# An RWKV layer and its FFN on one core: the last chunk of the opening is made in the FFN's own rows, its low parts by TensorE, with a new order of the first 32 tasks

## The chip, the cores and the metric

One core of one Trainium2 chip runs the whole program. The metric is the device time of one execution in microseconds (us); lower is better. Each kernel is executed several times, and one further execution is profiled. In that one the hardware profiler writes down when each instruction of each engine began and ended.

## The reference

There are two parts. A recurrence over 768 tokens runs for 4 batches and 8 heads of 48 channels; its output, 3072 tokens by 384 channels, is the input `x` of a feed-forward network (FFN) with 2048 hidden channels.

```python
def _attn_ref(r, k, v, w, u):
    ...
    for t in range(S):
        kt, vt, rt, wt = (k[:, :, t], v[:, :, t], r[:, :, t], w[:, :, t])
        cur = np.einsum('bhd,bhe->bhde', u[None] * kt, vt)
        y[:, :, t] = np.einsum('bhd,bhde->bhe', rt, state + cur)
        state = wt[:, :, :, None] * state + np.einsum('bhd,bhe->bhde', kt, vt)

def _moe_ref(x, w_in, w_out):
    h = x @ w_in
    g = h * (1.0 / (1.0 + np.exp(-1.702 * h)))
    return (g @ w_out).astype(np.float32)
```

## The kernel before

**Chunks.** The recurrence is cut into 24 chunks of 128 tokens, six to a batch. A chunk (`chunk(t)`, one `a` token of the order a step) takes these steps. VectorE makes running products of the decays, forward (`pm`) and backward (`li`), by two scans, and from them the scaled keys and queries `kf` and `qf` (both in the tile `kq`). TensorE makes the diagonal term (`ps_d`, from the product `rku` of r and k), the transposed keys (`ps_t`), the state's increment (`ps_u`), the scores (`ps_e` or `ps_s`) and the output `ps_y`. That output is the sum of a product of the queries with the state (L460) and a product of the masked scores `am` with the values (L507). `split` then writes the output into the FFN's input tile `x` as a high part (ScalarE, L229) and a low part (VectorE, L230, the output less its high part). ScalarE also squares `lp` (both running products) and `kq` and adds them up (`measure`, L235; the `m` tokens); the sums are tested at the end, and a guarded slow path runs if a value is out of range. `convert` (the `w` tokens) turns a fetched megabyte of 64-bit weights into a pair of a high and a low part: two ScalarE steps (L209, L210), two VectorE steps (L212, L215), one ScalarE step (L218), one VectorE step (L220).

**Tasks.** The FFN works through 96 tasks: six groups of four chunks (512 tokens), each with 16 slices of 128 hidden channels. A task j has a first product `g` of nine matmuls (three row blocks, each high by high, high by low, low by high), a gelu `h` on ScalarE and VectorE, and a second product `y` of nine matmuls into three accumulators `po`. The first product's result `ph` has two banks, so the task after the next waits until a gelu has read its bank.

**Rows.** An output `ps_y` has 112 rows: two heads of 48 channels with 16 rows between them, for four pairs of heads. The FFN wants three blocks of 128 rows. `fill_x` (the `x` tokens) closes that gap with six DMAs of 16 rows each inside `x` (L526), three issued by SyncE (SP) and three by GpSimd (POOL) in the opening.

**Order.** Nothing is scheduled by a tool. The string `RAMP` lists all steps of the first 32 tasks, and each engine gets its instructions in that order; `rest()` does the same for the steady part by the table `PARTS`. In `RAMP`, a token is a letter and a number: `l` loads a chunk, `f` fetches weights, `M` writes small constants, and `kN` issues N dummy matmuls on zeros (`keep_clock`, L602), which keep TensorE active. SyncE's queue takes its DMAs in that order too; `behind_moves` makes the DMAs issued after the six moves wait until the moves have landed.

Of the kernel before, what the change touches and what calls it, by code (L numbers as in the profile page):

```python
# [8 lines left out]
F32 = mybir.dt.float32  # L9
# [5 lines left out]
ALU = mybir.AluOpType  # L15
# [37 lines left out]
PARTS = [("a", 0, 0), ("a", 1, 0), ("a", 2, 0), ("m", 2, 0), ("a", 2, 1), ("a", 3, 0), ("m", 3, 0), ("a", 3, 1), ("a", 4, 1),  # L53
         ("a", 4, 1), ("l", 5, 0), ("l", 5, 0), ("a", 5, 1), ("a", 5, 1), ("a", 8, 1), ("a", 8, 1), ("x", 8, 1)]
BEFORE = 11

# [19 lines left out]
HALF = 14  # L76
WP = NF * DM // NL
# [8 lines left out]
def rwkv_ffn_kernel(ctx: ExitStack, tc, wkr, vp, vrk, ub, w_in, w_out, masks, vt, uc, out):  # L86
# [35 lines left out]
    later_b = later.bitcast(I32).unsqueeze(1).broadcast_to([P, NP, HB])  # L122
    u_heads = hm[:, 2:].rearrange("r (p h) -> r p h", h=2)
# [77 lines left out]
    def convert(i, pool, clamp):  # L201
# [6 lines left out]
        sums = {} if clamp else dict(accum_out=acc[:, 2 * NT + i : 2 * NT + i + 1])  # L208
# [43 lines left out]
    def token_halves(t, kf, qf, kt, v, s, sf):  # L252
# [78 lines left out]
        for b, y in enumerate(ps):  # L331
            split(*(xs[i][0:R2, n_, :, cols][:, :, half[b]] for n_ in range(2)), y)
# [3 lines left out]
    def chunk(t):  # L336
# [23 lines left out]
        if t < WHOLE:  # L360
            rk = at.tile([R2, NP, C], F32, tag="rku", name="rku")
# [11 lines left out]
        measures[t] = measured(t, lp, kq)  # L373
# [6 lines left out]
        if t < WHOLE:  # L380
            V.tensor_copy(s, ps_d.rearrange("p n h -> p (n h)"))
# [82 lines left out]

        if t < CHUNKS[0]:
# [458 lines left out]
```

## Time and profile before

| what | value |
|---|---|
| time, median of 3 runs | 502.7 us (502.22 to 502.75) |
| the profiled execution's own time | 502.98 us |
| its span in the trace | 501.2 us, 1.78 us less than its own time |
| busy: TensorE (PE) / VectorE (DVE) / ScalarE (ACT) / GpSimd (POOL) | 490.2 / 285.0 / 279.7 / 82.3 us |
| instructions in the trace | 12797 |
| dummy matmuls in the order | 79 |

The profile lists PE (matmuls), PEld (weight loads), DVE, ACT and POOL; a name with a q (SPq) is the engine's queue issuing a DMA. A span of the trace is a little shorter than the time of its execution, so sums made in the trace are carried over to the execution's own time, and from there to the median of the runs.

### The profile page before, as it was taken

To read this page: it belongs to the slowest core of one execution; us is meant where nothing else is said; L and a number is where in the kernel's file an instruction comes from. 1 tells how busy PE (TensorE), PEld (TensorE's weight loads), DVE (VectorE), ACT (ScalarE), POOL (GpSimd) and SP (SyncE) were. 2 spreads that over 40 slices of the span, in tenths; PEclk is the share of its full clock that TensorE was granted. 3 is DMA by queue.
4 is the path that set the end of the run, shared out by engine and by line. 5 is a ranking of instruction groups with operands and counts; after the bars stand their busy time and mean duration, and the time that the engine had idled before them with its cause. 6 is when DMAs were issued, how large, how long until landed. Compare 5 with 4: busy or idle time off the path is not lost.

```text
span 501.2 us, 12797 instructions
## 1 busy us (share of the span) xinstructions
PE 490.2 (98%) x5192; PEld 408.5 (81%) x5192; DVE 285.0 (57%) x460; ACT 279.7 (56%) x625; POOL 82.3 (16%) x173
## 2 busy tenths in 40 slices
PE   8998999999999999999999999999999999999995
PEld 3775888888888888888888888888888888888884
DVE  7889989988988423655555555555555322111110
ACT  4988897797856742554544554544554523323322
POOL 3004000002000020083205183205150002100000
PEclk9999999999999999999999999999999999999999
DMA  8865985043553320063113262113240001100001
GB/s 284 275 217 182 266 262 193 1 111 115 177 136 96 105 69 1 1 186 87 46 36 66 65 190 83 49 32 66 65 142 21 3 1 33 64 1 2 1 1 69
DMA packets 22018, 47.62 MB, mean 95 GB/s; under 512 B 4736, under 2 KB 11968, under 8 KB 21952
## 3 DMA queue, kind: packets, MB, share of 16 engines
q1 hardware_dynamic: 15120, 30.25, 19.5%
q0 software_dynamic: 6432, 15.95, 11.6%
q8 instruction: 43, 0.70, 0.6%
q10 hardware_dynamic: 400, 0.53, 0.3%
q14 instruction: 23, 0.19, 0.1%
HBM read 39.63 MB, written 4.72 MB: 88 GB/s over the span
## 4 chain that ended last, share of the span: by engine, by line
PE 95%; ACT 1%; DVE 1%; DMA 1%; issue 0%; POOL 0%; SPq 0%; ACTq 0%; POOLq 0%
PE po L613 26%; PE ph L613 24%; PE ph L555 5%; PE po L587 5%; PE ph L557 4%; PE ph L556 4%; PE po L589 4%; PE po L588 4%; PE idle L602 3%; PE ps_c L300 3%; PE ps_s L453 2%; PE ps_c L486 2%; PE ps_d L378 1%; PE ps_u L435 1%; PE ps_a L273 1%; PE ps_a L279 1%
## 5 line engine op out<-in xcount | busy, mean ns | idle before, releaser
L613 PE MATMUL ph<-x,pair 64*128 64x512 f32 x1134 | 185.3, 376 | 0.0
L573 DVE TENSOR_TENSOR gl<-gf,gh 128x512 fp32r<-128x512 f32 x96 | 66.3, 691 | 179.4 <-ACT gf L572 175.1
L613 PE MATMUL po<-gh,pair 64*128 64x512 f32 x768 | 157.0, 385 | 0.2 <-SPq L618 0.2
L613 PEld LDWEIGHTS ph<-x,pair 64*128 64x128 f32 x1134 | 143.3, 186 | 14.5
L572 ACT ACTIVATE gh<-ph 128x512 fp32r<-128x512 f32 x84 | 50.2, 598 | 162.3 <-PE ph L613 140.9
L613 PEld LDWEIGHTS po<-gh,pair 64*128 64x128 f32 x768 | 94.4, 186 | 10.8 <-issue 0.8
L613 PE MATMUL po<-gl,pair 64*128 64x512 f32 x384 | 98.0, 376 | 0.0
L526 POOL DMA_DIRECT2D x<-x x33 | 16.6, 509 | 245.1 <-DVE x L230 245.0
L613 PEld LDWEIGHTS po<-gl,pair 64*128 64x128 f32 x384 | 48.8, 186 | 5.0
L572 ACT ACTIVATE gf<-ph 128x512 f32<-128x512 f32 x84 | 49.9, 594 | 0.0
L555 PE MATMUL ph<-x,pair 128*128 128x512 f32 x99 | 39.4, 398 | 1.4 <-DMA x<-x 1.4
L557 PE MATMUL ph<-x,pair 128*128 128x512 f32 x99 | 38.0, 383 | 0.0
L556 PE MATMUL ph<-x,pair 128*128 128x512 f32 x99 | 37.9, 383 | 0.0
L587 PE MATMUL po<-gh,pair 128*128 128x512 f32 x96 | 37.8, 394 | 0.0
L589 PE MATMUL po<-gl,pair 128*128 128x512 f32 x96 | 36.8, 383 | 0.0
L588 PE MATMUL po<-gh,pair 128*128 128x512 f32 x96 | 36.8, 383 | 0.0
L424 ACT ACTIVATE am<-ident,s 128x128 f32<-128x128 f32 x112 | 34.2, 393 | 0.1
L235 ACT ACTIVATE junk<-lp 112x1032 bf16<-112x1032 f32 x24 | 25.6, 1069 | 12.7 <-DVE lp L355 12.7
L349 DVE TENSOR_TENSOR_SCAN lp<-wkr_t,d1r 112x516 f32<-112x516 f32 x24 | 29.5, 1228 | 1.5 <-DMA wkr_t<-in_wkr 1.3
L355 DVE TENSOR_TENSOR_SCAN lp<-wkr_t,d1f 112x516 f32<-112x516 f32 x24 | 29.4, 1226 | 0.3
L171 POOL DMA_DIRECT2D wkr_t<-in_wkr x54 | 27.0, 504 | 5.5 <-issue 3.2
L235 ACT ACTIVATE junk<-kq 112x1024 bf16<-112x1024 f32 x24 | 25.5, 1064 | 1.2 <-DVE kq L371 1.1
(110 smaller groups left out, 664.2 us busy)
## 6 DMA issues: line engine op xcount, KB each, us to landing
raw<-in_w_out SPq DMA_DIRECT2D x6, 1024.0 KB, 7.8
raw<-in_w_in SPq DMA_DIRECT2D x5, 1024.0 KB, 5.9
rk_t<-in_vrk POOLq DMA_DIRECT2D x9, 384.0 KB, 3.6
wkr_t<-in_wkr SPq DMA_DIRECT2D x4, 770.5 KB, 6.9
out_t<-ob POOLq DMA_DIRECT2D x12, 256.0 KB, 2.8
v_t<-in_vrk SPq DMA_DIRECT2D x15, 192.0 KB, 3.3
rk_t<-in_vrk SPq DMA_DIRECT2D x7, 384.0 KB, 3.6
x<-x POOLq DMA_DIRECT2D x33, 64.0 KB, 2.5
```

Source lines behind the costliest of these rows:

```text
L235: A.activation(junk[:, 0 : x.shape[1]], x, AF.Square, accum_out=acc[0:R2, i : i + 1])
L349: V.tensor_tensor_scan(li.rearrange("r p c -> r (p c)")[:, ::-1], w1[:, ::-1], d1r.rearrange("r p c -> r (p c)")[:, ::-1], 0.0, op0=ALU.mu ...
L424: A.activation(x_[:, p], ident, AF.Copy, scale=s[:, j : j + 1])
L555: T.matmul(o, h_, halves(x[:, 0, c, cs], plain), start=c == 0, stop=False)
L556: T.matmul(o, h_, halves(x[:, 1, c, cs], plain), start=False, stop=False)
L557: T.matmul(o, l_, halves(x[:, 0, c, cs], plain), start=False, stop=c == NM - 1)
L572: A.activation(g, ph, AF.Gelu_apprx_sigmoid, scale=1.0 / W_SCALE)
L573: V.tensor_tensor(gl, gf, gh.bitcast(F32), op=ALU.subtract)
L587: T.matmul(o, h_, halves(gh, plain), start=first, stop=False, skip_group_check=True)
L588: T.matmul(o, l_, halves(gh, plain), start=False, stop=False, skip_group_check=True)
L589: T.matmul(o, h_, halves(gl, plain), start=False, stop=f == NF - 1, skip_group_check=True)
L613: mm = T.matmul(by_twos(out), w[rows], halves(x[rows]), start=start, stop=stop, skip_group_check=True)
```

## The change

The outputs of chunk 3, the fourth and last of the first group, are made in the FFN's three blocks of 128 rows at once. The operands get padded copies (`spare`): seven copies on GpSimd move the values and the state into them, and `straight` issues 12 matmuls for the state and 12 for the scores, where there were 8 and 8. So only chunks 0 to 2 are moved by DMA, and the six moves (`x2` in place of `x3`) are issued when chunk 2 is written.

For chunks 0 to 3 the low part no longer comes from VectorE. TensorE adds the product of the high part with minus the identity (`minus`) to the output in PSUM, and ScalarE copies what is left. Of the FFN's first product of task 0 the nine matmuls stand in another order: three with the high part of `x`, three with low weights and the high part, then three with the low part.

The squares of `kq` go. In their place the copy of the high part adds up its row (`accum_out`), and the sums are tested for finite values at the end. The squares of `lp` of chunks 0 to 3 go too; a new generator `decays` loads the decays of these chunks again in the steady part (tasks 40 to 68), scans them again and adds up the squares. The copy of `ps_d` to `s` moves from VectorE to ScalarE. `RAMP` is written anew, with 48 dummies.

```diff
-PARTS = [("a", 0, 0), ("a", 1, 0), ("a", 2, 0), ("m", 2, 0), ("a", 2, 1), ("a", 3, 0), ("m", 3, 0), ("a", 3, 1), ("a", 4, 1),
+PARTS = [("a", 0, 0), ("a", 1, 0), ("a", 2, 0), ("m", 2, 0), ("a", 2, 1), ("a", 3, 0), ("a", 3, 1), ("a", 4, 1),
...
-k2 a2 a2 f2 l5 a3 w0 a3 a2 a3 a3 w0 a3 a2 a3 w1 x3 m3 l4 f4 w0 w0 a4 a4 w3 w2 k21 g0 f5 a4 g1 h0 a4 w2 m4 h1 a4
+a2 a2 a1 w0 k4 a2 k2 a3 a3 f6 x2 a4 a3 w2 w2 a3 a4 k1 a4 a3 f4 w1 k5 g0 m4 w2 w2 g1 h0 f3 h1 w1 w1 a4 a4 f5 w3 l5 w3
...
+THIRDS = [(m, (2 * m + i) * TOP // D, (2 * m + i) * TOP % D, i == 0) for m in range(NM) for i in range(2)]
...
-    def split(hi, lo, f):
-        A.copy(hi, f)
+    def split(hi, lo, f, to=None):
+        if to is None:
+            A.copy(hi, f)
+        else:
+            A.activation(hi, f, AF.Copy, accum_out=acc_x[0 : f.shape[0], to : to + 1])
         V.tensor_tensor(lo, f, hi.bitcast(F32), op=ALU.subtract)
...
+    def decays(t):
+
+        n = NP * CW
+        w = at.tile([R2, n + 1], F32, tag="rku", name="again")[0:R]
+        queue[0].dma_start(w, wkr[t, :, 0 : n + 1])
+        yield
...
+        V.tensor_tensor_scan(
+            flat[:, ::-1], w[:, 1:][:, ::-1], d1r[0:R].rearrange("r p c -> r (p c)")[:, ::-1], 0.0,
+            op0=ALU.mult, op1=ALU.add,
+        )
+        V.reciprocal(d1f[0:R, :, 0:1], li[:, :, 0:1])
+        yield
+        A.activation(flat, flat, AF.Square, accum_out=acc_lp[0:R, t : t + 1])
...
-        measures[t] = measured(t, lp, kq)
+        measures[t] = measured(t, lp)
...
-            V.tensor_copy(s, ps_d.rearrange("p n h -> p (n h)"))
+            A.copy(s, ps_d.rearrange("p n h -> p (n h)"))
...
+        def straight(ps, pair, low, high, rhs):
+
+            for m in range(NM):
+                for h in range(2):
+                    yield ps[h * HB : (h + 1) * HB, m], pair(m, h), rhs(m, h)
+            for m, h, d0, up in THIRDS:
+                out_, w_ = (ps[P - 2 * TOP :, m], high) if up else (ps[0:TOP, m], low)
+                yield out_, w_(m, h, d0), rhs(NM, h)
...
+                ):
+                    G.tensor_copy(dst, src)
...
-        split(x[0:R2, 0, :, cs], x[0:R2, 1, :, cs], ps)
...
+        A.activation(hi, ps, AF.Copy, accum_out=acc_x[0 : ps.shape[0], 2 * t : 2 * t + 1])
         state.pop(t - 1, None)
+        yield
+        n = ps.shape[0]
+        T.matmul(ps, minus[0:n, 0:n], hi, start=False, stop=True, skip_group_check=True)
+        A.copy(lo, ps)
         yield
...
+        terms = [(c, *n_) for c in range(NM) for n_ in ((0, 0), (0, 1), (1, 0))]
+        if j == 0:
+            terms = [(c, *n_) for n_ in ((0, 0), (1, 0), (0, 1)) for c in range(NM)]
...
-                if col == CHUNKS[group] - 1:
+                if col == CHUNKS[group] - 1 - (group == 0):
                     fill_x(xs[group], 0, (col + 1) * C)
...
+            for k in range(CHUNKS[0]):
+                for at_ in (1, 5, 6, 7, 8):
+                    plan.setdefault(2 * (LATE + 8 * k) + at_, []).append(f"e{k}")
...
+    V.tensor_scalar(acc_x, acc_x, 0.0, 0.0, op0=ALU.mult, op1=ALU.is_equal)
```

On TensorE, this is the end of the opening before: the last output products of chunk 3, then 21 dummies (one load and one matmul of them are shown), then the first product of task 0 (`ph`).

```order
L460 MATMUL ps_y<-kq,sf 48x128
L507 MATMUL ps_y<-am,v_t 64x128
L507 MATMUL ps_y<-am,v_t 48x128
...
L602 LDWEIGHTS d1r
L602 MATMUL idle<-d1r 128x512
...
L555 MATMUL ph<-x,pair_539 128x512
L556 MATMUL ph<-x,pair_539 128x512
L557 MATMUL ph<-x,pair_539 128x512
```

And this is the same place on TensorE in the change; `spare` holds the padded copies, L599 is the product with minus the identity, and five dummies stand ahead of the first products of tasks 0 and 1 (L641, 18 matmuls).

```order
L532 MATMUL ps_y<-kq,spare 64x128 x6
L532 MATMUL ps_y<-kq,spare 32x128
...
L577 MATMUL ps_y<-am,spare 64x128 x6
L577 MATMUL ps_y<-am,spare 32x128
L577 MATMUL ps_y<-am,v_t 16x128
...
L412 MATMUL ps_d<-hm,rku 128x2 x4
L599 MATMUL ps_y<-x,minus 128x384
L686 LDWEIGHTS d1r
L686 MATMUL idle<-d1r 128x512
...
L641 MATMUL ph<-x,pair_452 128x512 x18
L438 MATMUL ps_t<-ident,kq 128x112 x4
```

The 21 dummies have become five, the diagonal product of chunk 4 (`ps_d`) has moved ahead of task 0, and the product with `minus` is new.

On VectorE, this is what stands before from the last masking of chunk 3's scores to the work on chunk 4; `x<-ps_y` are the low parts of chunks 2 and 3, `raw`, `c` and `pair` belong to the weights.

```order
L471 COPY_PREDICATED am<-after,ps_s_485 128x512
L212 SCALAR_TENSOR_TENSOR raw_350<-raw_350 128x1024
L215 SCALAR_TENSOR_TENSOR c<-c,raw_350 128x1024
L230 TENSOR_TENSOR x<-ps_y,x 112x4x128 x2
L220 TENSOR_TENSOR pair_381<-c,pair_381 128x1024
L220 TENSOR_TENSOR pair_539<-c,pair_539 128x1024
L349 SCALAR_TENSOR_TENSOR lp<-wkr_t,d1r 112x516
```

In the change VectorE has this there, from the first scan of chunk 4 (L383) to the low part of the third weight (`pair_574`).

```order
L383 SCALAR_TENSOR_TENSOR lp<-wkr_t,d1r 112x516
L387 RECIPROCAL d1f<-lp 112x4
L230 TENSOR_TENSOR pair_452<-c,pair_452 128x1024
L538 COPY_PREDICATED am<-after,ps_s_458 128x512
L538 COPY_PREDICATED am<-after,ps_s_459 128x512
L389 SCALAR_TENSOR_TENSOR lp<-wkr_t,d1f 112x516
L396 TENSOR_TENSOR rku<-wkr_t 112x512
L222 SCALAR_TENSOR_TENSOR raw_408<-raw_408 128x1024
L225 SCALAR_TENSOR_TENSOR c<-c,raw_408 128x1024
L404 TENSOR_TENSOR kq<-wkr_t,lp 112x512
L405 SCALAR_TENSOR_TENSOR kq<-wkr_t,live,lp 112x512
L222 SCALAR_TENSOR_TENSOR raw_313<-raw_313 128x1024
```

The low parts of `x` are gone from VectorE, one weight in place of two is finished ahead of task 0, and the scan of chunk 4 has moved ahead of chunk 3's masking.

On SyncE's queue the opening begins like this before (`wkr_t` are decays, keys and queries, `v_t` values, `raw` weights):

```order
L164 DMA wkr_t<-in_wkr 96x517
L164 DMA wkr_t<-in_wkr 128x517
L164 DMA wkr_t<-in_wkr 96x1024
L174 DMA v_t<-in_vrk 128x384
L164 DMA wkr_t<-in_wkr 128x1024
L198 DMA raw_178<-in_w_out 128x2x1024
```

And like this in the change:

```order
L174 DMA wkr_t<-in_wkr 96x517
L174 DMA wkr_t<-in_wkr 96x1024
L174 DMA wkr_t<-in_wkr 128x517
L201 DMA raw_148<-in_w_in 112x2x1024
L174 DMA wkr_t<-in_wkr 128x1024
L184 DMA v_t<-in_vrk 128x384
```

A fetch of 896 KB of weights now stands ahead of chunk 1's keys and queries and of chunk 0's values.

## Rows read from the trace of the kernel before

**Rows 1.** The page: the chain that ended last, by engine.

```profile
PE 95%; ACT 1%; DVE 1%; DMA 1%; issue 0%; POOL 0%; SPq 0%; ACTq 0%; POOLq 0%
```

**Rows 2.** Waits of TensorE, the FFN's: us in total, times, longest.

```profile
PE ph L555 <- DMA x<-x: 1.4, 2, 1.1
```

**Rows 3.** Timeline of TensorE at task 0: start, us, engine, line, operation.

```profile
36.00 1.09 PE L507 MATMUL ps_y<-am,v_t 128*64 128x128 f32 x16
37.02 4.71 PE L602 MATMUL idle<-d1r 112*128 112x512 bf16 x21
42.81 0.47 PE L555 MATMUL ph<-x,pair 128*128 128x512 f32 x1 [1.08 <-DMA x<-x]
...
44.02 0.47 PE L555 MATMUL ph<-x,pair 128*128 128x512 f32 x1 [0.28 <-DMA x<-x]
```

**Rows 4.** The chain that ended last, opening to 48 us.

```profile
38.57 1.21 DVE x L230 x2
39.79 0.76 SPq L526
40.60 3.29 DMA x<-x
...
47.69 0.79 PE ps_d L378 x8
```

**Rows 5.** Timeline of VectorE: one chunk, then its neighbours.

```profile
3.84 1.23 DVE L349 TENSOR_TENSOR_SCAN lp<-wkr_t,d1r 112x516 f32<-112x516 f32 x1 [1.27 <-DMA wkr_t<-in_wkr]
...
16.60 1.23 DVE L349 TENSOR_TENSOR_SCAN lp<-wkr_t,d1r 112x516 f32<-112x516 f32 x1
...
18.08 1.23 DVE L355 TENSOR_TENSOR_SCAN lp<-wkr_t,d1f 112x516 f32<-112x516 f32 x1
...
19.81 0.68 DVE L370 TENSOR_TENSOR kq<-wkr_t,lp 112x512 f32<-112x512 f32 x1
20.41 0.74 DVE L371 SCALAR_TENSOR_TENSOR kq<-wkr_t,live,lp 112x512 f32<-112x512 f32 x1
21.34 1.23 DVE L212 SCALAR_TENSOR_TENSOR raw<-raw 128x1024 int32<-128x1024 int32 x1 [0.18 <-ACT c L210]
...
23.75 0.35 DVE L441 TENSOR_TENSOR sf<-ps_u,sf 112x192 f32<-112x192 f32 x1
...
24.41 1.34 DVE L471 COPY_PREDICATED am<-after,ps_e 128x512 f32<-128x512 int32 x2
25.64 1.22 DVE L349 TENSOR_TENSOR_SCAN lp<-wkr_t,d1r 112x516 f32<-112x516 f32 x1
...
39.68 2.35 DVE L220 TENSOR_TENSOR pair<-c,pair 128x1024 fp32r<-128x1024 f32 x2
```

**Rows 6.** Timeline of ScalarE: the high part of chunk 3.

```profile
37.17 0.58 ACT L229 CAST x<-ps_y 112x512 fp32r<-112x512 f32 x1 [0.66 <-PE ps_y L507]
```

**Rows 7.** Busy time by stretch: us, then PE, PEld, DVE, ACT, POOL, granted clock, DMA.

```profile
43.00:160.00 117.00, 116.72 (x833) 97.16 (x833) 106.36 (x152) 91.97 (x187) 5.21 (x10) 1.00 0.54 162
300.00:400.00 100.00, 99.28 (x1494) 84.67 (x1492) 53.22 (x101) 51.30 (x132) 23.77 (x47) 1.00 0.22 58
```

**Rows 8.** Timelines of GpSimd, and of VectorE at the second place.

```profile
2.39 0.29 POOL masks.py:199 TENSOR_SCALAR_AFFINE_SELECT ident<-ident 128x128 f32<-128x128 f32 x1
...
41.81 1.44 POOL L735 TENSOR_SCALAR_AFFINE_SELECT eye<-eye 64x64 f32<-64x64 f32 x2
...
41.95 1.27 DVE L349 TENSOR_TENSOR_SCAN lp<-wkr_t,d1r 112x516 f32<-112x516 f32 x1
```

**Rows 9.** DMA issues to 62 us: size, median us from issue to landing.

```profile
raw<-in_w_in SPq DMA_DIRECT2D x1, 896.0 KB, 7.8
wkr_t<-in_wkr SPq DMA_DIRECT2D x1, 512.0 KB, 6.1
```

**Rows 10.** Timeline of TensorE: dummies before and after 7.4 us.

```profile
3.59 1.91 PE L602 MATMUL idle<-d1r 112*128 112x512 bf16 x4
...
8.77 1.03 PE L602 MATMUL idle<-d1r 112*128 112x512 bf16 x4
```

More of the change, by code (lines that the diff above doesn't have):

```diff
@@ L122, in rwkv_ffn_kernel @@
     later_b = later.bitcast(I32).unsqueeze(1).broadcast_to([P, NP, HB])
+    spare = wt.tile([P, 2 * WP], F32, tag=f"w{2 * NL - 1}", name="spare")
+    minus = wt.tile([P, P], F32R, tag=f"w{2 * NL - 2}", name="minus")
+    padded, at_ = [], 0
+    for n, w in ((P, P), (P, 2 * TOP), (R2, D + 2 * TOP), (R2, TOP), (R2, 2 * TOP)):
+        padded.append(spare[0:n, at_ : at_ + NM * w].rearrange("p (m w) -> p m w", m=NM))
+        at_ += NM * w
     u_heads = hm[:, 2:].rearrange("r (p h) -> r p h", h=2)
@@ L207, in convert @@
         cf = c.bitcast(F32)
-        sums = {} if clamp else dict(accum_out=acc[:, 2 * NT + i : 2 * NT + i + 1])
+        sums = {} if clamp else dict(accum_out=acc_sum[:, i : i + 1])
         A.activation(l, l.bitcast(U32), AF.Copy, scale=L_SCALE)
@@ L331, in token_halves @@
         for b, y in enumerate(ps):
-            split(*(xs[i][0:R2, n_, :, cols][:, :, half[b]] for n_ in range(2)), y)
+            split(*(xs[i][0:R2, n_, :, cols][:, :, half[b]] for n_ in range(2)), y, 2 * t + b)
         state.pop(t - 1, None)
@@ L494, in chunk @@
             for b, y in enumerate(ps):
-                split(*(xs[i][0:R2, n_, 2 * b : 2 * b + 2, cs] for n_ in range(2)), y)
+                split(*(xs[i][0:R2, n_, 2 * b : 2 * b + 2, cs] for n_ in range(2)), y, 2 * t + b)
             state.pop(t - 1, None)
@@ L503, in chunk @@
         ps = ps_y
-        for p in range(NP):
+        if t == CHUNKS[0] - 1:
+            for out_, w_, x_ in straight(
+                ps, lambda m, h: vz[:, m, h * HB : (h + 1) * HB],
+                lambda m, h, d0: three[:, h * D + d0 : h * D + d0 + TOP],
+                lambda m, h, d0: vh[:, (h * D + d0) // (2 * TOP)], lambda p, h: am[h][:, p],
+            ):
+                T.matmul(out_, w_, x_, start=False, stop=False, skip_group_check=True)
+        for p in range(NP if t != CHUNKS[0] - 1 else 0):
             for h in range(2):
@@ L508, in chunk @@
                     ps[head(h), p], v[:, c : c + HB - h * TOP], am[h][:, p],
-                    start=sf is None and p == 0, stop=p == NP - 1, skip_group_check=True,
+                    start=sf is None and p == 0, stop=t >= CHUNKS[0] and p == NP - 1, skip_group_check=True,
                 )
@@ L514, in chunk @@
             xs[i] = new_x(i)
-        x = xs[i]
-        split(x[0:R2, 0, :, cs], x[0:R2, 1, :, cs], ps)
+        hi, lo = (xs[i][0 : ps.shape[0], n_, 0 : ps.shape[1], cs] for n_ in range(2))
+        if t >= CHUNKS[0]:
+            split(hi, lo, ps, 2 * t)
+            state.pop(t - 1, None)
+            yield
+            return
+        A.activation(hi, ps, AF.Copy, accum_out=acc_x[0 : ps.shape[0], 2 * t : 2 * t + 1])
         state.pop(t - 1, None)
+        yield
+        n = ps.shape[0]
+        T.matmul(ps, minus[0:n, 0:n], hi, start=False, stop=True, skip_group_check=True)
+        A.copy(lo, ps)
         yield
@@ L552, in first_product @@
         x = xs[i]
-        for c in range(NM):
-            h_, l_ = weight(0, f, c)
-            T.matmul(o, h_, halves(x[:, 0, c, cs], plain), start=c == 0, stop=False)
-            T.matmul(o, h_, halves(x[:, 1, c, cs], plain), start=False, stop=False)
-            T.matmul(o, l_, halves(x[:, 0, c, cs], plain), start=False, stop=c == NM - 1)
+        terms = [(c, *n_) for c in range(NM) for n_ in ((0, 0), (0, 1), (1, 0))]
+        if j == 0:
+            terms = [(c, *n_) for n_ in ((0, 0), (1, 0), (0, 1)) for c in range(NM)]
+        for k_, (c, w_, x_) in enumerate(terms):
+            pair = tuple(weight(0, f, c))
+            T.matmul(o, pair[w_], halves(x[:, x_, c, cs], plain), start=k_ == 0, stop=k_ == 3 * NM - 1)
         parts[j] = ph
```

85 lines of the change are left out of this document (59 added, 26 removed).

## The prediction

> **What bounds the kernel now.** I read the chain that ended last first: TensorE holds 95% of it [rows 1], so an edit helps only where it shortens TensorE's list or a wait in it. Next come TensorE's waits: after the start the FFN's only waits are 1.4 us for the DMAs inside `x`, in two pieces [rows 2]. That understates what they cost, since 21 dummy matmuls (4.71 us) stand ahead of them and do no work [rows 3]. From 43 to 160 us TensorE is busy for 116.72 of 117 us, from 300 to 400 us for 99.28 of 100 [rows 7]. So the end is the moment at which task 0 starts, plus a list that runs nearly without a gap. The whole question is when task 0 starts, and whether the list behind it stays closed.
>
> Task 0's fourth matmul starts at 44.02 us, after its wait [rows 3]; three matmuls at the pace of the dummies (4.71 / 21 = 0.224 us) precede it, so without gaps the task would have begun at 43.35 us. The chain shows why: the low parts of chunks 2 and 3 on VectorE end at 39.78 us, SyncE issues for 0.76 us, a DMA takes 3.29 us [rows 4].
>
> **The new start of task 0.** Three things now gate it: VectorE's list, TensorE's last steps, and the six moves. I sum VectorE's list by starts of neighbours in the timeline, which leaves out overlaps [rows 5].
> - A chunk from its first scan to the end of `qf`: 16.60 to 20.41 + 0.74, 4.55 us. Its first scan and reciprocal alone: 18.08 - 16.60 = 1.48. The second scan and the product `rku`: 19.81 - 18.08 = 1.73.
> - Masking: 25.64 - 24.41 = 1.23. A step on the state: 0.35 at most.
> - A weight's two VectorE steps: 23.75 - 21.34 = 2.41; its low part 2.35 / 2 = 1.18.
>
> In the changed order, up to `rku` of chunk 4, stand four chunks (18.20), four maskings (4.92), six state steps (2.10), chunk 4's two scans with `rku` (1.48 + 1.73) and one weight (2.41 + 1.18): 32.0 us. The four low parts, the four copies of `ps_d` and a second weight are gone from ahead of it. The first scan begins at 3.84 us, so the list ends at 35.8 us without a wait. I allow 0.3 us for waits, little, because the copies that waited for `ps_d` have left VectorE: 36.1 us.
>
> On TensorE `ps_d` of chunk 4 follows (0.79 [rows 4]): 36.9. Chunk 3's masking ends 1.73 us ahead of `rku`, at 34.4; its 12 products (8 took 1.02 us, from 36.00 to 37.02 [rows 3], so 12 take 1.53) and the high part (0.58 [rows 6]) end at 36.5, in time. The product with `minus` and five dummies (6 x 0.224 = 1.34) end at 38.3.
>
> The moves: chunk 2 is masked when 26.1 of VectorE's 32.0 us are done (four chunks, three maskings, five state steps, two weight steps), so at 30.2. Products 1.0, high part 0.6, product with `minus` 0.2, two low parts on ScalarE 1.2, rests 0.2: 33.4. In the old kernel the second block arrived 4.24 us after the split (39.78 to 44.02 [rows 3, 4]), and the third no later than 4.9. So the blocks are there between 37.6 and 38.3, while the third matmul asks at 38.3 + 0.45. I take **38.4 us** for the start: 43.35 - 38.4 = 4.95 us earlier.
>
> **What else moves.** `ps_d` of chunk 4 stood behind task 0 and 1 and cost 0.79 us of the closed list; it now lies ahead of task 0, in front of work that has to wait anyway. Together 5.7 us.
>
> Costs that no row prices: the product with `minus` has 512 or 384 columns like a dummy, 0.224 us; at the least nothing, at the most four times that (+0.7). The copy of `s` on ScalarE, and the accumulator's read behind a sum, lie each between nothing and the 0.58 us of a copy of 512 columns [rows 6]; I take nothing, because ScalarE also loses the squares of `kq`.
>
> The seven GpSimd copies: nearest rows are a select of 128x128 with 0.29 us early on, and two of 64x64 that took 1.44 us while VectorE ran without a rest [rows 8]. So 0.3 to 0.7 each; I take 0.7. Five of them follow the state's last step (22.4 us of VectorE's list, so 26.5): 26.5 + 3.5 = 30.0, needed at about 33. Hidden; at twice that price they would add 0.5 us. The Trainium skill (SBUF — State Buffer, Who interferes with whom) says that GpSimd and VectorE share one pair of ports under an exclusive lock, and that a VectorE instruction with two SBUF inputs and a GpSimd one that reads SBUF block each other fully. By that rule either side may wait: if VectorE lost, seven copies of 0.3 us would put 2.1 us on its list. The trace bears out the half in which GpSimd loses: the select was slow, while VectorE's scan that began at 41.95 took 1.27 us, beside 1.23 for another [rows 5, 8].
>
> The decays come back four times in the steady part: two scans and a reciprocal (1.48 + 1.23, about 2.7 us of VectorE) and two squares each. VectorE is busy there for 53.22 of 100 us and ScalarE for 51.30 [rows 7]: nothing; without that cover it would be 4 x 2.7 = 11 us. The list behind task 0 feeds on VectorE, which is busy for 106.36 of 117 us [rows 7], and there the new start could be paid for. At its start the old kernel owed chunk 4's second scan to `qf` (3.1 us) and a third weight (3.6); the new one owes `kf` and `qf` (1.3), one weight's two steps (2.4) and two low parts (2.4). That is 6.7 against 6.1, so VectorE stands no worse to TensorE than before. I charge 0.4 us for new small waits: the last group of moves in `RAMP` (`x11`) now has only one second product and a few attention products between it and the task that reads it.
>
> Net 5.3 us. Against the profiled execution's own time: 502.98 - 5.3 = 497.7; the median of the runs shown is 0.28 lower, so **497.4 us**.
>
> **Rivals.**
> 1. *The opening starts later* (16 in 100). 896 KB of weights now go out ahead of chunk 1's keys and queries, which took 6.1 us (512 KB) from issue to landing. A transfer of 896 KB took 7.8 us, so 384 KB more cost 1.7 [rows 9]; by that ratio 896 KB in front delay them by 4.0 us at most, and by nothing if both run at once. VectorE asks for them at 11.1 (3.84 + 4.55 + 1.48 + 1.23); what it feels of the delay is less by the time that they came early, which no row tells. Seven GpSimd copies of 0.3 us that hold VectorE up (2.1 us) would add to it. 1 to 3 us of the gain are lost: 498.4 to 500.4.
> 2. *Given back behind task 0* (10 in 100). `y0` now stands behind four first products, and its weight's low part comes late. By my sums it is ready at 45.8 us (36.1, two weights' two steps 4.8, `kf` and `qf` 1.3, a low part 1.2, two gelu differences as long as a `kf`, 0.6 each, and the last low part 1.2), and `y0` starts at 38.4 + 36 x 0.224 = 46.5 at the earliest: 0.7 us of room. If VectorE is 3 us later, 2 us are lost there: 499 to 501.
> 3. *The moves gate as before* (5 in 100). If chunk 2's low part comes only when ScalarE is through a weight's steps, the moves land at 42 to 43 us and nothing is won: 501.8 to 502.7.
> 4. *Slower: TensorE's clock* (7 in 100). The granted clock reads 1.00 in every stretch [rows 7], but the pace tells the level: from 3.59 us four dummies took 1.91 us, from 8.77 us four took 1.03 [rows 10], so 512 columns at 1.2 and then at 2.4 GHz. Until the rise TensorE did nothing but dummies. The new order starts with 10 in place of 20, so TensorE rests before chunk 0's first product is ready. If the lower level lasts or returns, work on TensorE in the opening takes twice as long. It decides from the point at which over 6.3 us of it on the path run at 1.2 GHz: 503.7 us, and 504 is my figure for it. Against it: the new list has few rests after 12 us. The Trainium skill (TensorE: Matmul & The Clock Gate, Part 1) says that the lower rate is the default and activity releases it. By that rule a rest can bring the lower rate back; that it starts low these two rows bear out, and a fall no run here shows.
>
> **How the numbers follow.** My forecast has 62 in 100, with its own range of 496.2 to 498.6. About 1 us (0.2%) is what a measurement of this kernel can tell from no change. Faster by more than that are the forecast and the first two rivals: 88; within it the third: 5; slower the fourth: 7. To leave out no more than 2 in 10 the range takes in the first rival and most of the second: 495.7 to 500.6. Its low end is a start of task 0 at 36.9, without any rest in VectorE's list and fewer microseconds behind it.
>
> **What would show it.** In the changed profile task 0's first matmul should start near 38.4 us, with no wait for `x<-x` over 0.5 us; `rku` of chunk 4 on VectorE should end near 36; the GpSimd copies should end by 31; TensorE should stay busy for over 99% from 40 to 200 us; the scans of `li_again` should leave no wait of TensorE's near them. The prediction is wrong if TensorE waits for `ps_y` or `gh` for microseconds, or if dummies after 10 us pace at 0.43 us.

## The result, and the profile after

The changed kernel is slower: 506.8 us median of 4 runs (506.36 to 507.25), where the kernel before took 502.73 (502.22 to 503.04, 4 runs on the same chip). The ratio is 1.0082, 95% interval 1.0064 to 1.0099. The profiled execution took 506.55 us, its span is 504.8 us (501.2 before). The prediction was 497.4 us, with a range to 500.6.

Task 0 starts at 45.81 us, 7.4 us later than predicted and 2.46 us later than the 43.35 us worked out for the kernel before. This is TensorE's timeline in the changed kernel (start, us, engine, line, operation):

```profile
8.25 1.67 PE L686 MATMUL idle<-d1r 112*128 112x512 bf16 x7
13.60 1.06 PE L469 MATMUL ps_u<-v_t,kt 128*64 128x48 f32 x16 [3.67 <-DMA v_t<-in_vrk]
14.59 2.08 PE L487 MATMUL ps_e<-kq 64*128 64x128 f32 x16
...
23.84 1.16 PE L487 MATMUL ps_e<-kq 64*128 64x128 f32 x16
...
40.46 1.65 PE L532 MATMUL ps_y<-kq,spare 64*64 64x128 f32 x24
42.03 1.10 PE L577 MATMUL ps_y<-am,spare 128*64 128x128 f32 x13
...
43.84 0.95 PE L412 MATMUL ps_d<-hm,rku 112*128 112x2 f32 x8
...
44.91 1.25 PE L686 MATMUL idle<-d1r 112*128 112x512 bf16 x5
45.81 4.45 PE L641 MATMUL ph<-x,pair 128*128 128x512 f32 x18
```

Two things are to be seen. TensorE has done its first 17 dummies (ten, then seven) at 9.9 us and then rests for 3.67 us, until chunk 0's values are there. And a chunk's score products (eight, which the trace writes down as 16 instructions) take 2.08 us behind that rest, for chunk 0, and 1.16 us later on, for chunk 1. The windows of the same kernel (us; then PE, PEld, DVE, ACT, POOL, granted clock, DMA) say why:

```profile
12.00:13.00 1.00, 0.00 (x0) 0.00 (x0) 0.04 (x1) 0.00 (x0) 0.00 (x0) 0.90 0.98 325
13.00:14.00 1.00, 0.40 (x9) 0.43 (x11) 1.00 (x2) 0.00 (x0) 0.00 (x0) 0.50 0.93 352
...
21.00:22.00 1.00, 1.00 (x7) 0.20 (x6) 0.00 (x0) 1.00 (x5) 0.00 (x0) 0.50 0.91 360
22.00:23.00 1.00, 1.00 (x21) 1.00 (x21) 0.00 (x0) 1.00 (x2) 0.00 (x0) 0.50 0.17 70
23.00:24.00 1.00, 1.00 (x17) 0.83 (x15) 0.99 (x2) 1.00 (x2) 0.00 (x0) 0.98 0.09 25
```

The granted clock falls to 0.50, the level of 1.2 GHz, near the end of the rest (0.90 is the mean from 12 to 13 us), and is back at 2.4 GHz at 23 us. The rest itself comes from SyncE's queue. The chain that ended last has the values' transfer in it, and the DMA issues of the first 45 us give the size and the median us to landing of the two transfers ahead of it:

```profile
3.19 10.27 DMA v_t<-in_vrk
```

```profile
raw<-in_w_in SPq DMA_DIRECT2D x1, 896.0 KB, 8.5
wkr_t<-in_wkr SPq DMA_DIRECT2D x1, 512.0 KB, 10.2
```

The values, 192 KB, were issued at 3.19 us and landed at 13.46, behind 896 KB of weights and chunk 1's 512 KB; these 512 KB took 10.2 us where they took 6.1 before [rows 9]. VectorE's waits follow (its timeline):

```profile
12.96 0.69 DVE L396 TENSOR_TENSOR rku<-wkr_t 112x512 f32<-112x512 f32 x1 [2.08 <-DMA wkr_t<-in_wkr]
...
16.70 1.33 DVE L538 COPY_PREDICATED am<-after,ps_e 128x512 f32<-128x512 int32 x2 [1.22 <-PE ps_e L487]
...
23.01 0.36 DVE L475 TENSOR_TENSOR sf<-ps_u,sf 112x192 f32<-112x192 f32 x1 [3.66 <-PE ps_u L469]
...
39.08 1.33 DVE L538 COPY_PREDICATED am<-after,ps_s 128x512 f32<-128x512 int32 x2
...
41.44 0.66 DVE L396 TENSOR_TENSOR rku<-wkr_t 112x512 f32<-112x512 f32 x1
```

With 0.20 us more, it waited 7.16 us: first for the keys and queries, then for products that TensorE made at 1.2 GHz. `rku` of chunk 4 ends at 42.1 us, predicted 36.1, and TensorE takes it up (`ps_d`, L412) only at 43.84.

The rest went mostly as predicted. The moves hold task 0 up no more. GpSimd's copies (timeline) end at 35.8 us, and TensorE reads them from 40.46 us on:

```profile
26.34 0.73 POOL L520 COPY spare<-v_t 128x288 f32<-128x288 f32 x2 [20.03 <-DMA v_t<-in_vrk]
32.93 1.17 POOL L520 COPY spare<-sf 112x144 f32<-112x144 f32 x1 [5.86 <-DVE sf L423]
34.05 1.76 POOL L526 COPY spare<-sf 64x32 f32<-64x32 f32 x4
```

Behind task 0, TensorE's waits hold two small new ones, for the moves of the second group and for the test at the end:

```profile
PE ph L641 <- DMA x<-x: 0.6, 1, 0.6
...
PE ps_n L903 <- DVE oks L901: 0.3, 1, 0.3
```

The distance between the two kernels, before and changed, at each task, read from the gelu's `gf` on ScalarE, is 2.57 us at task 0, 2.24 at task 34 and 2.64 at task 76; it steps to 3.31 at task 77, where the test's product stands, and ends at 3.40.

### The profile page after: what moved, and what is told of

Same layout as the page of the kernel before. It is cut to its first block, busy times and chain, and to the rows that moved or that the text cites. A ratio compares the mean times of both kernels' runs of the same rounds, so it can differ in the third digit from the quotient of the medians.

```text
span 504.8 us, 12795 instructions
## 1 busy us (share of the span) xinstructions
PE 489.8 (97%) x5181; PEld 409.4 (81%) x5181; DVE 291.7 (58%) x461; ACT 263.9 (52%) x641; POOL 88.6 (18%) x189
## 3 DMA queue, kind: packets, MB, share of 16 engines
q0 software_dynamic: 6688, 16.70, 11.9%
## 4 chain that ended last, share of the span: by engine, by line
PE 92%; DMA 3%; ACT 2%; DVE 1%; issue 1%; SPq 0%; POOL 0%; ACTq 0%
PE po L697 26%; PE ph L697 24%; PE ph L641 12%; PE po L671 4%; PE po L672 4%; PE po L673 4%; PE ps_c L334 3%; PE ps_s L487 2%; DMA v_t<-in_vrk 2%; PE idle L686 2%; PE ps_u L469 1%; PE ps_d L412 1%; PE ps_c L553 1%; PE ps_a L307 1%; PE ps_a L313 1%; PE ps_t L438 1%
## 5 line engine op out<-in xcount | busy, mean ns | idle before, releaser
L641 PE MATMUL ph<-x,pair 128*128 128x512 f32 x297 | 70.3, 387 | 0.6 <-DMA x<-x 0.6
L641 PEld LDWEIGHTS ph<-x,pair 128*128 128x128 f32 x297 | 55.2, 188 | 11.2 <-issue 2.1
L383 DVE TENSOR_TENSOR_SCAN lp<-wkr_t,d1r 112x516 f32<-112x516 f32 x24 | 29.4, 1226 | 1.2 <-DMA wkr_t<-in_wkr 1.0
L243 DVE TENSOR_TENSOR x<-ps_c,x 112x256 fp32r<-112x256 f32 x36 | 14.1, 423 | 18.0 <-ACT x L242 18.0
L242 ACT ACTIVATE x<-ps_c 112x256 fp32r<-112x256 f32 x36 | 13.4, 380 | 18.3 <-PE ps_c L334 10.2
L249 ACT ACTIVATE junk<-lp 112x1032 bf16<-112x1032 f32 x20 | 21.3, 1066 | 1.5 <-DVE lp L389 1.4
```

The lines of the kernel that those rows point to most:

```text
L249: A.activation(junk[0:n], x, AF.Square, accum_out=acc_lp[0:n, t : t + 1])
L383: V.tensor_tensor_scan(li.rearrange("r p c -> r (p c)")[:, ::-1], w1[:, ::-1], d1r.rearrange("r p c -> r (p c)")[:, ::-1], 0.0, op0=ALU.mu ...
L641: T.matmul(o, pair[w_], halves(x[:, x_, c, cs], plain), start=k_ == 0, stop=k_ == 3 * NM - 1)
```

## The experiments

Theories of the first four runs. Q: SyncE's queue delays the opening, because a block of weights goes out ahead of what chunks 0 and 1 need. D: too few dummies; TensorE rests and its clock falls. B: time is lost behind task 0. The table has for each run the start of task 0 in its profiled execution (us), the median time of all its executions, and the recorded ratio to the kernel before on the same chip, which is not exactly the quotient of two medians. The kernel before had medians of 502.37 us beside runs 1 to 4, 502.51 beside 5 to 8, 502.59 beside 9 to 11 and 502.39 beside 12.

| run | task 0 | median us | ratio, 95% interval |
|---|---|---|---|
| the changed kernel | 45.81 | 506.8 | 1.0082 (1.0064 to 1.0099) |
| 1 weights later | 41.81 | 502.12 | 0.9992 (0.9972 to 1.0012) |
| 2 more dummies | 43.21 | 504.19 | 1.0035 (1.0013 to 1.0057) |
| 3 chunk 0's values first | 40.13 | 501.27 | 0.9974 (0.9957 to 0.9991) |
| 4 kernel before, weights first | 43.18, waits inside | 502.68 | 1.0003 (0.9990 to 1.0016) |
| 5 run 3, weights last | 41.25 | 501.85 | 0.9994 (0.9969 to 1.0018) |
| 6 run 3, five dummies fewer | 38.40 | 498.97 | 0.9946 (0.9925 to 0.9968) |
| 7 run 5, twelve dummies fewer | 40.48 | 501.17 | 0.9983 (0.9954 to 1.0012) |
| 8 run 7, no decays | 43.23 | 500.79 | 0.9977 (0.9939 to 1.0015) |
| 9 run 6, seven dummies fewer | 38.43 | 498.64 | 0.9912 (0.9894 to 0.9929) |
| 10 run 6, chunk 3 moved by DMA | 43.80 | 504.01 | 1.0016 (1.0002 to 1.0030) |
| 11 run 6, chunk 1's values early | 39.37 | 500.25 | 0.9970 (0.9941 to 0.9999) |
| 12 run 9, low parts on VectorE | 39.36, a wait inside | 502.33 | 0.9995 (0.9980 to 1.0011) |

**Run 1.** The first block of weights (`f0`) behind chunk 0's values and chunk 1's keys and queries.

```diff
-l0 l0 M a0 a0 l1 f0 a0 l1 l0 k10
+l0 l0 M a0 a0 l1 a0 l1 l0 f0 k10
```

> The changed kernel with one move: the 896 KB fetch of weights is issued behind chunk 1's keys and queries and chunk 0's values, not ahead of them. Theory Q (the place in SyncE's queue makes chunk 0's values and chunk 1's keys land late; TensorE's rest of 3.67 us and the lower clock follow from that): the values land before 11.5 us in place of 13.46, TensorE rests under 1.5 us there, the granted clock stays at 1.00 from 10 to 20 us, task 0 starts near 39.5 in place of 45.81, time near 500.5 us. Theory D (48 dummies are too few, the clock falls whatever the data do): the clock still falls between 10 and 22 us, task 0 starts after 43, time 504 or more. Theory B (the loss lies behind task 0): task 0 moves and the time does not, over 505.

**Run 2.** The changed kernel's queue, with 24 dummies in place of 7 behind chunk 0's steps (they stand ahead of the first `ps_u`).

```diff
-a1 l2 a0 l2 a0 k7 a0 a1
+a1 l2 a0 l2 a0 k24 a0 a1
```

> The changed kernel with 24 dummies in place of 7 ahead of chunk 0's state product, so that TensorE works through the wait for chunk 0's values; the queue stays as it is. Theory Q: the values still land near 13.5 us and chunk 1's keys near 12.9, so VectorE's 2.08 us of wait stays; the clock stays at 2.4 GHz, the five attention steps between 13.6 and 22 us take 4.5 in place of 8.3 us; task 0 near 42, time near 503. Theory D: nearly everything comes back, task 0 near 39.5, time near 500.5. Theory B: no change, over 505.

**Run 3.** Chunk 0's values ahead of chunk 1's keys and queries, and the weights behind both.

```diff
-l0 l0 M a0 a0 l1 f0 a0 l1 l0 k10
+l0 l0 M a0 a0 l1 a0 l0 l1 f0 k10
```

> As the first kernel of this call, and chunk 0's values also go out ahead of chunk 1's keys and queries. Theory Q: the values land near 9 us, chunk 1's keys and queries no later than 11.5; TensorE's rest there under 1 us, VectorE's wait under 0.5; time 0.3 us around that of the first kernel, near 500.3. Theory D: the clock falls all the same, 504 or more.

**Run 4.** The kernel before, with the block of weights in front.

```diff
-l0 l1 l0 a0 M l0 a0 a0 k20 a0 m0 m0 l1 a1 f1 l1
+l0 l1 l0 f1 a0 M l0 a0 a0 k20 a0 m0 m0 l1 a1 l1
```

> The kernel before with one move: its first fetch of 1 MB of weights is issued ahead of chunk 0's values and chunk 1's keys and queries. Theory Q: chunk 0's values and chunk 1's keys land 2 to 4 us later, TensorE waits for the values for 1 to 3 us, task 0 starts 1 to 3 us later, time 504 to 506. Theory D: 79 dummies keep the clock up and the rest is hidden, 502.7 as before.

What was measured. Moving one fetch by two places takes 4.7 us off the time (run 1), and the values in front 5.5 us (run 3): theory Q holds for the changed kernel. Its figures were too good: task 0 starts at 41.81 us in run 1, not near 39.5, because the seven dummies ahead of `ps_u` ran at half the pace there (3.19 us in place of 1.67), and run 3 took 501.27 us, not 500.3.

In the kernel before, a like fetch in front (1 MB) costs nothing (run 4), though the 512 KB then took 9.3 us to land. There `ps_u` starts at 12.19 us, as without it (12.25), behind 26 dummies, and the moves still gate task 0 (waits of 1.06 and 0.34 us). Run 4 is not the changed kernel's queue, though: chunk 0's values stand behind the fetch alone there, not behind chunk 1's 512 KB too, and 8.6 us after their issue at 2.68 us they had landed, ahead of the end of the dummies. That an early fetch hurts only where the order asks for the values at 9.9 us and has nothing to do until they come agrees with run 4; no run shows it by itself.

Run 2 separates the two costs. From the start of chunk 0's `ps_u` to task 0 it takes 27.88 us (15.33 to 43.21), the changed kernel 32.21 (13.60 to 45.81), although `ps_u` was later still. Both go through the same list on TensorE, and neither timeline shows a rest in it. Nearly all of the difference lies in the first products, up to the first output of chunk 0 (L581), which take 9.09 us in the changed kernel and 4.91 in run 2. TensorE's timelines, of the changed kernel and of run 2:

```profile
22.69 1.22 PE L581 MATMUL ps_y<-am,v_t 128*64 128x128 f32 x15
```

```profile
15.33 0.67 PE L469 MATMUL ps_u<-v_t,kt 128*64 128x48 f32 x16
...
20.24 1.05 PE L581 MATMUL ps_y<-am,v_t 128*64 128x128 f32 x15
...
43.21 4.44 PE L641 MATMUL ph<-x,pair 128*128 128x512 f32 x18
```

So 4.3 us of the changed kernel's opening are the clock. The cost that theory D names is real; its forecast for run 2 (39.5 and 500.5 us) is missed, and theory Q's (42 and 503) is nearer to the 43.21 and 504.19 measured. Dummies are no remedy for a wait, and here the clock fell in spite of them, so that the 24 took 7.03 us. Windows of run 2, columns as above:

```profile
9.00:10.00 1.00, 1.00 (x3) 0.30 (x2) 0.93 (x3) 1.00 (x5) 0.00 (x0) 0.50 1.04 251
...
13.00:14.00 1.00, 1.00 (x7) 0.45 (x5) 0.05 (x1) 0.00 (x0) 0.00 (x0) 1.00 0.92 321
```

Theory B is out: in all these runs the tasks keep the distance to the kernel before that task 0 has, within 1.2 us.

In run 3 chunk 0 runs through, and what was hidden behind it shows up (TensorE's timeline):

```profile
10.04 0.67 PE L469 MATMUL ps_u<-v_t,kt 128*64 128x48 f32 x16
...
16.70 0.58 PE L469 MATMUL ps_u<-v_t,kt 128*64 128x48 f32 x15 [2.18 <-DMA v_t<-in_vrk]
...
38.97 0.42 PE L599 MATMUL ps_y<-x,minus 128*128 128x384 f32 x1
39.23 1.25 PE L686 MATMUL idle<-d1r 112*128 112x512 bf16 x5
40.13 4.44 PE L641 MATMUL ph<-x,pair 128*128 128x512 f32 x18
```

TensorE waits for chunk 1's values, and from 16.70 us on has no rest, so its own list, dummies included, now runs up to task 0. `rku` of chunk 4 ends at 36.67 us on VectorE, but TensorE comes to it at 38.16 only. The next runs ask which of the two lists gates (T: TensorE's; V: VectorE's) and where the weights have to stand.

**Run 5.** As run 3, with chunk 1's values and chunk 2 also ahead of the weights.

```diff
-a0 l0 l1 f0 k10 a0 a0 a1 f0 a1 l2 a0 l2
+a0 l0 l1 l1 k10 a0 a0 a1 a1 l2 f0 f0 a0 l2
```

> As the run with chunk 0's values first, and in addition chunk 1's values and chunk 2's decays, keys and queries are asked for ahead of the first weights. That run still waited 2.18 us on TensorE for chunk 1's values and 1.22 and 0.36 us on VectorE, and task 0 began at 40.13. Theory Q (the place in SyncE's queue is what delays the opening): these waits go, `rku` of chunk 4 ends near 35.1 instead of 36.7 and task 0 begins 1.6 us earlier, near 38.5; some 499.7 us where that run had 501.3. Rival W (the weights are needed as early): their first step then waits 2 us or more, and task 0 begins at 40 or later.

Neither: the waits for chunks 1 and 2 go, but chunk 3's decays, keys and queries now stand behind the weights (a wait of 0.22 us on VectorE here, more in runs 7 and 8). In this execution the dummies of the opening also ran at half the pace for longer (`ps_u` at 12.63 us instead of 10.04), so the run says little of the queue.

**Run 6.** As run 3, without the five dummies ahead of task 0.

```diff
-f4 w1 k5 g0
+f4 w1 g0
```

> The run with chunk 0's values first, without the five dummies that stand between the last product with minus the identity and task 0. There the dummies took 39.23 to 40.13 and the low part was ready at 39.91; the first six matmuls of task 0 don't read it. Theory T (TensorE's own list, dummies included, gates task 0): task 0 begins 1.1 us earlier, near 39.1, and the time is 1.0 us lower, some 500.3 us. Theory V (the dummies only fill a wait, as the prediction had it): task 0 begins earlier but waits as long inside, for `x<-x` or the low part; no change of over 0.3 us.

Theory T. From the last product with `minus` to task 0 it is 0.26 us instead of 1.16. Inside the task one wait of 0.3 us for the moves is left (TensorE's weight loads, first line below): the last move lands 3.4 us after its issue at 35.68 us, behind the start of the task. The other 0.8 us by which task 0 comes earlier than in run 3 come from transfers that landed sooner (`ps_u` of chunk 1 at 15.86 instead of 16.70). TensorE's timeline of run 6 follows:

```profile
PEld ph L641 <- DMA x<-x: 0.3, 1, 0.3
```

```profile
38.14 0.42 PE L599 MATMUL ps_y<-x,minus 128*128 128x384 f32 x1
38.40 4.69 PE L641 MATMUL ph<-x,pair 128*128 128x512 f32 x18
```

Task 0 starts at the 38.4 us of the prediction, but not by its path: its sum had the five dummies in it (see below).

**Run 7.** Run 5 without these five, and without the seven around the products with `minus` of chunks 2 and 3.

```diff
-w0 k4 a2 k2 a3 a3 f6 x2 a4 a3 w2 w2 a3 a4 k1 a4 a3 f4 w1 k5 g0
+w0 a2 a3 a3 f6 x2 a4 a3 w2 w2 a3 a4 a4 a3 f4 w1 g0
```

> Both edits together, and without the seven dummies (4, 2 and 1) around the products with minus the identity of chunks 2 and 3 either. Theory T: TensorE had no rest from 16.7 us to task 0 in the run with the values first, so each dummy there that fills no wait counts 0.22 us: task 0 begins near 36.5 and the time is some 498 us. Theory V: `rku` of chunk 4 sets the end, near 35.1, and task 0 begins 2 us after it, near 37.2 (498.6 us). Rival C (the dummies hold TensorE's clock up): the granted clock falls under 0.95 in a stretch behind 30 us, and the time is above 501 us.

**Run 8.** Run 7 without the decays of the steady part (the range of chunks 0 to 3 is not tested).

```diff
-            for k in range(CHUNKS[0]):
+            for k in range(0):
```

> The kernel with fewer dummies, without the decays in the steady part: the squares of the running products of chunks 0 to 3 are left out, so that their range is not tested. Theory S (the decays cost time in the steady part, where the changed kernel's tasks fell 1.2 us further behind): 0.9 to 1.3 us less than the kernel with fewer dummies. Rival N (they are hidden, and the 1.2 us come from stores and from the test at the end): within 0.3 us of it.

Both inherit run 5's late keys: VectorE waits 3.16 us (run 7) and 2.56 us (run 8) for chunk 3's, TensorE rests, and the clock falls (a mean of 0.72 from 28 to 32 us in run 7, 0.50 in run 8). First TensorE's timeline of run 7, then of run 8:

```profile
27.00 1.02 PE L412 MATMUL ps_d<-hm,rku 112*128 112x2 f32 x8 [1.90 <-DVE rku L396]
...
30.74 2.08 PE L487 MATMUL ps_s<-kq 64*128 64x128 f32 x16
```

```profile
26.61 1.61 PE L412 MATMUL ps_d<-hm,rku 112*128 112x2 f32 x8 [1.80 <-DVE rku L396]
...
32.45 2.08 PE L487 MATMUL ps_s<-kq 64*128 64x128 f32 x16
```

That, with 501.17 us, is what rival C forecast. Run 5, which has all the dummies, has two executions of ten with a mean granted clock of 0.987 and 0.988 too (505.44 and 505.12 us), and run 9 below, without the seven but with the better queue, keeps the clock: so the late transfers and not the missing dummies are the likelier cause.

Run 7's ten executions give the clock's price within one kernel: four with a mean granted clock of 0.986 to 0.990 took 503.12 to 504.64 us, the six of 0.994 and more 498.97 to 501.47, medians 503.6 and 500.0. It is a price between longer and shorter falls, since the profiled one, whose clock fell too, is of the six. For the decays the medians say nothing, with so many fallen clocks; the traces do. From task 40 to task 80 the distance to the kernel before grows by 1.06 us with the decays (run 7) and by 1.05 without (run 8). Rival N: the decays are hidden, and 0.67 of these 1.06 us fall at the test's product, in every variant.

**Run 9.** Run 6 without the seven dummies of run 7's diff.

> The best run so far (chunk 0's values first, no dummies right ahead of task 0), also without the seven dummies (4, 2 and 1) around the products with minus the identity of chunks 2 and 3. In that run TensorE had no rest from 16 us to task 0 at 38.40, and `rku` of chunk 4 ended at 35.84. Theory T (TensorE's own list gates task 0): each of the seven that fills no wait counts 0.22 us; the products of chunk 3 then start when its masking ends (34.0), and task 0 begins near 37.0, 1.4 us less: 497.6 us. Theory V (VectorE gates, and the seven fill waits for ScalarE's high parts): no change of over 0.3 us. Rival C (the seven hold TensorE's clock up): 1.2 GHz level in a stretch ahead of task 0, and 502 us or more in executions where it falls.

The lowest time, 0.9912 of the kernel before, though its four executions and run 6's overlap (497.62 to 499.36 and 498.86 to 500.57 us). In the profiled executions its transfers were later than run 6's (`ps_u` of chunk 1 at 16.57 instead of 15.86) and task 0 starts at the same time: by that the seven gave some 0.7 us, half of theory T's 1.4; the medians, 0.3 us apart, don't show it. Rival C is out here: the clock stayed at 1.00 in every stretch from 4 to 44 us. Run 9's timelines of VectorE and TensorE:

```profile
35.85 0.67 DVE L396 TENSOR_TENSOR rku<-wkr_t 112x512 f32<-112x512 f32 x1
```

```profile
37.25 1.05 PE L412 MATMUL ps_d<-hm,rku 112*128 112x2 f32 x8
38.17 0.42 PE L599 MATMUL ps_y<-x,minus 128*128 128x384 f32 x1
38.43 4.26 PE L641 MATMUL ph<-x,pair 128*128 128x512 f32 x18
```

**Run 10.** Run 6 with the first part of the change undone: chunk 3 in rows of 112, moved by DMA.

```diff
-            last_one = t == CHUNKS[0] - 1
+            last_one = False
...
-                if col == CHUNKS[group] - 1 - (group == 0):
+                if col == CHUNKS[group] - 1:
...
-f6 x2 a4 a3 w2 w2 a3 a4 k1 a4 a3 f4 w1 g0
+f6 a4 a3 w2 w2 a3 a4 k1 a4 a3 x3 f4 w1 k20 g0
```

> The same best run, with chunk 3's outputs made in rows of 112 again and moved by DMA with the other chunks' (six moves behind its low part, 20 dummies ahead of task 0); the low parts by TensorE and the good order of SyncE's queue stay. Theory R (the outputs in the FFN's rows take the transfer out of the path): low part at 39.9, 0.76 us of issue and 3.29 us of transfer as in the kernel before, so task 0's last three matmuls wait until 43.9 or later, and the time is 4 to 5 us more, 503 to 504 us. Rival O (the gain comes from the new order of steps alone): within 1 us of the best run.

Theory R: 5.0 us more than run 6 between the medians, and no faster than the kernel before. In its timeline 20 dummies cover the moves, as in the kernel before [rows 3]; the chain that ended last goes through the moves (3.11 us from 41.27) and not through the dummies:

```profile
41.27 3.11 DMA x<-x
```

```profile
39.66 4.49 PE L686 MATMUL idle<-d1r 112*128 112x512 bf16 x20
43.80 5.01 PE L641 MATMUL ph<-x,pair 128*128 128x512 f32 x18
```

In the profiled executions, 5.6 us apart (504.50 and 498.89 us), about 1.2 us are not the moves': `ps_d` of chunk 4 starts at 38.51 us here and at 37.33 in run 6, with a clock that fell at 16 to 20 us in this execution.

**Run 11.** Run 6 with chunk 1's values two steps earlier.

```diff
-k10 a0 a0 a1 f0 a1 l2
+k10 a0 a0 l1 a1 f0 a1 l2
```

> The same best run, with chunk 1's values too asked for two steps earlier, ahead of the second block of weights and of chunk 2. Theory Q: TensorE's wait of 1.67 us at 15.86 and VectorE's of 0.38 us there go, chunk 2's decays come 0.5 us later at most; TensorE's list from there on starts 0.5 to 1 us earlier, task 0 near 37.7, 498.2 us. Rival W: chunk 2's decays, keys and queries come later by as much as is won; within 0.4 us of the best run.

The waits for them go, as Q says, but the time is no lower: chunk 0's `ps_u` starts at 12.42 us here (9.72 in run 6), because the first dummies ran at half the pace for longer. From there to task 0 it takes 26.95 us, in run 6 28.68. How much of these 1.7 us the values won, and how much is only slack behind a late start, this run can't tell; whether they would pay with an early rise stays open.

**Run 12.** Run 9 with the second part of the change undone: the low parts of chunks 0 to 3 on VectorE.

```diff
-        T.matmul(ps, minus[0:n, 0:n], hi, start=False, stop=True, skip_group_check=True)
-        A.copy(lo, ps)
+        V.tensor_tensor(lo, ps, hi.bitcast(F32), op=ALU.subtract)
```

> The run without the seven dummies, with the low parts of chunks 0 to 3 made on VectorE again (output less high part, 0.6 us each in the kernel before), in place of the product with minus the identity and ScalarE's copy. The outputs in the FFN's rows and the order of SyncE's queue stay. Theory V (VectorE's list is close behind TensorE's, so its relief by TensorE pays): three low parts stand ahead of `rku` of chunk 4 and one behind it, `rku` ends 1.8 us later, near 38.3, and task 0 begins 1 to 2 us later, 499.5 to 500.5 us. Rival T (TensorE's list sets task 0's start with 0.7 us to spare, and it loses three products of 0.2 us and a wait for ScalarE each): within 0.5 us of that run, or a little faster.

Theory V, and more: 3.7 us. `rku` ends 1.8 us later, as expected, but the larger loss is inside task 0, where chunk 3's low part stands in VectorE's list behind a weight's two steps and chunk 4's `kf` and `qf` (it starts at 41.95 us, `rku` ends at 38.34). So part of the 3.7 us is the place of that step; no run puts it further ahead:

```profile
39.36 1.63 PE L639 MATMUL ph<-x,pair 128*128 128x512 f32 x6
42.55 0.73 PE L639 MATMUL ph<-x,pair 128*128 128x512 f32 x2 [1.56 <-DVE x L598]
```

## Why the prediction was wrong

**The step that failed** is "I allow 0.3 us for waits, little, because the copies that waited for `ps_d` have left VectorE". VectorE's list itself was right: 38.54 us from its first scan to the end of `rku`, less 7.16 of waits, is 31.4 us, and the sum was 32.0. The waits were 7.16 us, and they came from SyncE's queue and TensorE's clock. They put the end of `rku` 6.0 us off (6.9 more of waits, 0.6 less of list, 0.3 for an earlier first scan).

**A second step failed by 1.4 us**: the one that puts behind chunk 3's masking only "its 12 products", which "end at 36.5, in time". The masking ends at 40.41 us; from 40.46 to 43.62 us TensorE makes both sets of 12, those of the state too, because its list had got no further. So it takes up `rku`, done at 42.10, at 43.84. Runs 3 and 6 show the same at full clock: 1.49 us from the end of `rku` to `ps_d`. TensorE's own list had no rest left, and the sum had only its last steps in it.

**Rivals 1 and 4 were one case.** The first had the right cause (896 KB ahead of chunk 1) but only chunk 1's keys in its price; the values of chunk 0, which stand behind both, were not in it, and they were the worst. The fourth had the right mechanism, but its condition was not met: it asked for over 6.3 us of work at the lower level, and the work that ran at it from 13.6 to 22.7 us is 4.9 us at the higher one (run 2), a loss of 4.2. By that rival's own sum (497.4 and 4.2 more) the clock alone would have left the kernel faster than before; with the late values it was slower. That rival also spoke against itself with "the new list has few rests after 12 us": the late values make the rest, at 9.9 to 13.6 us. Taken apart the two had 16 and 7 in 100; in this kernel they come together: all four executions of the changed kernel have a mean granted clock of 0.992 or less, all ten of run 3, without the long rest, 0.994 or more. That the rest brings the fall is likely, not shown: in run 2 the clock fell without it.

**The 7.4 us between 38.4 and 45.81**, by the runs: 4.3 for the clock (run 2), 1.4 more for chunk 0's late values (45.81 - 40.13 in run 3, less 4.3), and 1.7 that run 3 still has. Run 6 gave 1.7 back, 0.9 of it by leaving out the five dummies and 0.8 because chunk 1's values landed sooner than in run 3. The five dummies were costed as cover for a wait, 1.1 us, and there was little left to cover: the first six matmuls of task 0 do not read the low part, and of the moves 0.3 us were left (run 6).

**What was right, and what by luck.** That task 0 starts at 38.40 and 38.43 us in runs 6 and 9, where the sum said 38.4, is in part luck: the sum has the five dummies in it, 1.12 us, which these runs don't have, and lacks the 1.49 us (run 6) by which TensorE comes late to `ps_d`. What holds of it is the length of VectorE's list and that the moves gate no more (rival 3 out), but with little to spare: the last lands near 39.1 us in run 6, where 38.3 was forecast, and near 38.6 in run 9, so a start of task 0 that is earlier still would meet them. Both parts of the change carry the gain: without the new rows 5.0 us are lost (run 10), without TensorE's low parts 3.7 (run 12), each with the reserve named there. `y0` waits for nothing, in runs 6 and 9 either, so rival 2 is out. The seven copies on GpSimd took 3.66 us where 4.9 were allowed, and hid; the decays cost nothing (run 8). The Trainium skill (SBUF — State Buffer, Who interferes with whom) says that a VectorE instruction with two SBUF inputs and a GpSimd one that reads SBUF contend. Run 3 agrees: a product that takes 0.68 us took 0.91 beside a copy; the changed kernel's VectorE shows no slower instruction beside the copies.

**What was missing behind task 0.** The test's product, now exposed, took 0.67 us, and the moves of the second group 0.6, where 0.4 was charged for all new small waits. These 0.9 us more explain most of why run 9, with the predicted start, took 498.64 us and not 497.4.

**Left open.** Why the distance grows by a further 0.4 us or so in the steady part was not traced to one instruction. No run held the clock up with the queue as it was: that the clock's fall makes the 4.3 us rests on run 2, whose list is the same, and on the two groups of run 7.

## What to carry to other kernels

Where an order is rewritten to ask for something earlier, add up what each queue has ahead of that request in bytes, and for the operand needed first, not only for the one that was moved. Price a wait of TensorE twice: the wait, and the work behind it at the lower clock if the rest lets it fall; here the second was the larger (4.3 us, beside a rest of 3.67). Sum the lists of all engines up to the same point, not only the one that gated before. And when a wait is taken away, the dummies that covered it turn into work on the path: count them again.

## What was not expected of the hardware

- A rest of the same length lets the clock fall in one execution and not in another: 2.15 us in run 9 and 2.18 in run 3 without a fall, 2.13 us at the same place in run 10 with one (0.58 granted from 16 to 20 us), 1.80 us in run 8 with one. In run 2 it fell between 8 and 9 us (0.91 granted there, 0.50 in the next) while TensorE had been busy since 7.04. The Trainium skill (TensorE: Matmul & The Clock Gate, Part 1) has the lower rate as the default that activity lifts; the changed kernel's 13 to 23 us agree that it can come back in mid-kernel.
- The first rise differs between executions of nearly the same opening: seven dummies took 1.67 us from 8.25 us in the changed kernel, and 3.19 us from 9.51 in run 1, with a granted clock of 1.00 in the record of both. The pace tells, not the record.
- A small transfer pays for what stands ahead of it: 192 KB of values took 10.27 us to landing behind 1408 KB issued just ahead of them on SyncE's queue, and 4.6 us in run 3, where they stand ahead of both; the median of the 15 such transfers on that queue is 2.8 us.
